# Hourglass attention and a gated MLP: the last value chunk of batch 0 on another DMA queue, shorter filler matmuls, and the first weights in smaller transfers

## The chip, the core and the metric

The kernel runs on one core of a Trainium2 chip. The core has a matmul engine (TensorE, PE in the profile; its weight loads are PEld), three engines for elementwise work (VectorE or DVE, ScalarE or ACT, GpSimd or POOL), and SyncE (SP), which here only issues transfers. Each engine works through its own list of instructions in order. Sixteen DMA engines move data between HBM and SBUF, the memory on the chip; matmuls write PSUM, from which VectorE and ScalarE read. GpSimd's transfers can convert fp32 to bf16 on the way; SP's copy as they are.

The metric is the device time of one execution in microseconds. The kernel before has a median of 316.63 us in three runs (315.98 to 320.5).

## The reference

Eight batches of eight heads, 576 tokens, head size 64. Attention is the sum of two parts: one over the means of four neighbouring tokens, repeated fourfold, and one over tokens less than four apart. An MLP follows.

```python
def _attn_ref(q, k, v):
    q_d = q.reshape(B, H, Sd, factor, D).mean(axis=3)      # factor = 4; k_d, v_d alike
    out_d = sm_attn(q_d, k_d, v_d)
    out_up = np.repeat(out_d, factor, axis=2)
    mask = np.abs(pos[:, None] - pos[None, :]) < factor
    scores = np.where(mask, scale * np.matmul(q, k.transpose(0, 1, 3, 2)), -1000000000.0)
...
    return out_up + np.matmul(attn, v)

def _moe_ref(x, w_in, w_out):                              # x: 4608 x 512, d_ff = 2048
    h = x @ w_in
    g = h * (1.0 / (1.0 + np.exp(-1.702 * h)))
    return g @ w_out
```

## The kernel before

The 4608 tokens form nine groups of 512 for the MLP. For each group `mm1` (line 697) multiplies by w_in (line 682) and applies the gate with ScalarE, and `mm2` (line 714) multiplies by w_out (line 746) and stores the result. Attention of the next batch is cut into steps and put between the matmuls of the running group at written-out positions, so that from about 24 us on TensorE has a full list. Batch 0 has no such cover: its attention is written out ahead of the loop, lines 789 to 878, and the order of the lines is the order on every engine.

This opening is what the change touches. In its order:

- GpSimd issues the loads of q and k of batch 0 (`load_1`, two tiles each), then the values (`load_vb`, line 219: five chunks of 128 rows, each in two halves of 64 partitions, fp32 in HBM to bf16 in the tile `vb`), then w_in in four transfers of 512 columns (`load_w_in`), of which the first stands ahead of the rest of the opening and three behind `pool_qk`, then q and k of batch 1, the first half of w_out, and inside group 0 the values of batch 1 and the second half of w_out.
- TensorE first runs filler matmuls on zeros (`warm`, line 637: `n` matmuls of `cols` columns; with `z=wf` on an fp32 tile, where one matmul shows as two passes in the profile, otherwise bf16). Then come the local scores of head group 0 (`scores`, line 367), fillers, those of head group 1, the downsampled scores (line 379), fillers, `prep_vd_pe` (line 336: sums of four value rows by matmuls with the selection matrix `psel`; its first call needs chunks 0 to 3, its second chunks 3 and 4), and the products with the values: `av_local0` (line 511, all five chunks) and `av_down0` (lines 525, 534). The turn of the result into the layout of the MLP is `turned` (lines 576 and 587, with a copy by ScalarE), and then the first matmuls with w_in follow (line 682).
- VectorE turns q and k (`prep_1`, line 267), sums fours (line 286) and normalises (`normalise0`, lines 553 to 561).
- ScalarE builds `psel` (`end_psel`, lines 173 to 178), takes the exponentials (`exp_local`, line 417; `exp_down`, line 423), copies the sums of values (line 345) and the turned results (lines 599, 603).
- SP issues nothing until batch 2's values (`load_v`, line 203: fp32 into a tile `vf`, converted by an engine with `prep_v`, line 305). `load_v` takes a gate: a small copy into the tile that an engine makes first, so that the transfers, which write the same place, wait for it.

The tile `vb` of batch 0 also holds a column of ones, set by `fill`, so that the product gives the sums for the division.

Of the kernel before, what the change touches and what calls it, by code (L numbers as in the profile page):

```python
# [19 lines left out]
def kernel(  # L20
# [9 lines left out]
    nc = tc.nc  # L30
# [38 lines left out]
    PM = [psum.tile([128, 512], FP32, name=f"pm{i}") for i in range(2)]  # L69
# [8 lines left out]
    def pm_tile():  # L78
        turn["m"] += 1
        return PM[turn["m"] % 2]  # L80

    wz = consts.tile([128, 512], BF16, name="wz")
    wf = consts.tile([128, 512], FP32, name="wf")
    off = consts.tile([128, 60], BF16, name="off")
    psel = consts.tile([128, 7, 64], BF16, name="psel")
# [27 lines left out]
    def fill():  # L113
        nc.vector.memset(wz, 0.0)
        nc.vector.memset(wf, 0.0)
        for t in kdT:
            nc.vector.memset(t[:, SD:160, :], 0.0)
        for t in vbs:
            nc.vector.memset(t[:, :, :, 64:65], 1.0)
        for t in vds:  # L120
            nc.vector.memset(t[:, :, :, 64:65], 4.0)
        for t in es:
            nc.vector.memset(t[:, :, 300:304], 1.0)
        for t in eds:
            nc.vector.memset(t[:, :, 432:480], 1.0)


    def make_off():
        nc.vector.tensor_tensor(out=dm, in0=dm, in1=dm, op=ALU.mult)
        nc.vector.tensor_single_scalar(out=dm, in_=dm, scalar=9.5, op=ALU.is_lt)  # L130
        nc.vector.tensor_scalar(
            out=off, in0=dm, scalar1=-1.0, scalar2=1e6, op0=ALU.add, op1=ALU.mult
        )
# [13 lines left out]
    def make_bias():  # L147
        nc.vector.memset(bias[:, 3:4], -3.0)
        nc.vector.tensor_copy(out=bias[:, 0:2], in_=rv)
        nc.vector.tensor_scalar(  # L150
            out=bias[:, 0:2], in0=bias[:, 0:2], scalar1=-1.0, scalar2=400.0,
            op0=ALU.add, op1=ALU.mult,
        )
# [17 lines left out]
    def end_psel():  # L171
        for m in range(7):
            nc.scalar.activation(
                out=dp[:, m], in_=di[:, 0:64], func=AF.Abs, scale=8.0, bias=db[:, m : m + 1]
            )
        nc.scalar.activation(out=dp, in_=dp, func=AF.Relu, bias=bias[:, 3:4])
        for sl, c in ((slice(0, 1), 1), (slice(1, 7), 0)):
            nc.scalar.activation(
                out=psel[:, sl], in_=dp[:, sl],
                func=AF.Exp, scale=-400.0, bias=bias[:, c : c + 1],  # L180
            )
# [21 lines left out]
    def load_v(b, gate=None, chunks=range(5)):  # L203
        t = ldp.tile([128, 5, H, D], FP32, name="vf", tag="vf")
        vf[b] = t
        if gate is not None:
            gate(t[0:1, 0, 0, 0:1])
        for i in chunks:
            for par in range(2):
                nc.sync.dma_start(  # L210
                    out=t[64 * par : 64 * par + 64, i],
                    in_=bass.AP(
                        tensor=v.tensor,
                        offset=v[b, 0].offset + (114 * i + KSTART[par]) * D,
                        ap=[[D, 64], [S * D, H], [1, D]],
                    ),
                )

    def load_vb(b, i):
        for par in range(2):  # L220
            nc.gpsimd.dma_start(  # L221
                out=vbs[b % 2][64 * par : 64 * par + 64, i, :, 0:D],
                in_=bass.AP(
                    tensor=v.tensor,
                    offset=v[b, 0].offset + (114 * i + KSTART[par]) * D,
                    ap=[[D, 64], [S * D, H], [1, D]],
                ),
            )
# [13 lines left out]
    def load_w_in(c, n):  # L242
        nc.gpsimd.dma_start(
            out=w_in_bf[:, :, c : c + n],
            in_=bass.AP(
                tensor=moe_w_in.tensor, offset=moe_w_in.offset + c,
                ap=[[d_ff, 128], [128 * d_ff, n_dmc], [1, n]],
            ),
        )
# [13 lines left out]
    def prep_1(name, b, qd):  # L263
        store, dst = {"k": (kf, kT), "q": (qf, qT)}[name]
        tt = work.tile([128, S, 2], BF16, name=f"{name}T{qd}", tag=f"{name}T{qd}", bufs=1)
        t32 = tt.rearrange("p t a -> p (t a)").bitcast(FP32)
        nc.vector.transpose(  # L267
            out=t32.rearrange("p (i c) -> p c i", c=18),
            in_=store[b, qd].bitcast(FP32).rearrange("p (c d) -> p c d", c=18),
        )  # L270
        dst[b, qd] = tt
# [10 lines left out]
    def reduce_qk(b, qd, name):  # L282
        t = kdT[qd][:, 0:SD, :] if name == "k" else new_qdT(b, qd)
        src = (kT if name == "k" else qT)[b, qd]
        with nc.allow_low_precision("the sum is rounded once, as the pairwise one is"):
            nc.vector.tensor_reduce(
                out=t, in_=src.rearrange("p (j f) a -> p j a f", f=4),
                axis=mybir.AxisListType.X, op=ALU.add,
            )
# [15 lines left out]
    def prep_v(b, eng, i=slice(0, 5), h=slice(0, H)):  # L305
        cp = eng.copy if eng is nc.scalar else eng.tensor_copy
        cp(out=vbs[b % 2][:, i, h, 0:D], in_=vf[b][:, i, h])  # L307
# [17 lines left out]
    def prep_vd_pe(b, pv, kcs=range(3), between=None):  # L325
        hp0, n = 0, HP
        vb, vd = vbs[b % 2], vds[b % 2]
        for kc, iis in ((0, (0, 1)), (1, (1, 2, 3)), (2, (3, 4))):
            if kc not in kcs:
                continue  # L330
            c0 = 256 * (kc - kcs[0])
            if between and kc == 1:
                between()
            for i in iis:
                for j in range(2):
                    nc.tensor.matmul(
                        pv[64 * j : 64 * j + 64, c0 : c0 + D * n],
                        lhsT=psel[:, PSEL.index((i, kc)), :],
                        rhs=vb[:, i, :, :].rearrange(
                            "p (hp j) d -> p hp j d", j=2  # L340
                        )[:, hp0 : hp0 + n, j, 0:D],
                        start=(i == iis[0]), stop=(i == iis[-1]),
                        tile_position=(0, 64 * j),
                    )
        nc.scalar.copy(
            out=vd[:, kcs[0] : kcs[-1] + 1, :, 0:D],
            in_=pv[:, 0 : 256 * len(kcs)].rearrange(
                "p (k h d) -> p k h d", k=len(kcs), h=HP
            ),
        )  # L350
# [26 lines left out]
    def score_d(b, qd, sd, kc, a, r):  # L377
        rows, j = slice(32 * r, 32 * r + 32), r % 2
        nc.tensor.matmul(  # L379
            sd[64 * j : 64 * j + 64, r // 2, SD * kc : SD * kc + SD],  # L380
            lhsT=kdT[qd][rows, 48 * kc : 48 * kc + 64, a],
            rhs=qdT[b, qd][rows, :, a],
            start=(a == 0), stop=(a == 1),
            tile_position=(32 * r, 64 * j),
        )
# [10 lines left out]
    def scores_d(b, qd, sd):  # L396
        for kc in range(3):
            for a in range(2):
                for r in range(4):
                    score_d(b, qd, sd, kc, a, r)  # L400
        return sd
# [13 lines left out]
    def exp_local(qd, sp):  # L415
        for u in range(2):
            nc.scalar.activation(  # L417
                out=es[2 * qd + u][:, :, 0:300], in_=sp[u][:, :, 0:300],
                func=AF.Exp, scale=inv_sqrt_d,
            )  # L420

    def exp_down(qd, sd):
        nc.scalar.activation(
            out=eds[qd][:, :, 0:432], in_=sd[:, :, 0:432],
            func=AF.Exp, scale=inv_sqrt_d / 16.0,
        )
# [210 lines left out]
    def warm(n, cols=512, t=None, z=wz):  # L637
        t = pm_tile() if t is None else t
        for _ in range(n):
            nc.tensor.matmul(  # L640
                t[:, 0:cols], lhsT=z[:, 0:128], rhs=z[:, 0:cols], start=True, stop=True
            )
# [150 lines left out]
    load_1("q", q, qf, 0, 1)  # L793
    iota_psel()
    fill()
    for i in range(5):
        load_vb(0, i)
    load_w_in(0, 512)
    warm(3, z=wf)
    warm(2)  # L800
    make_off()
    make_ident(di)
    make_psel()
    make_bias()
    end_psel()
    prep_1("k", 0, 0)
    prep_1("q", 0, 0)
    sp = scores(0, 0, PA[0:2])
# [4 lines left out]
    reduce_qk(0, 0, "q")  # L813
    pool_qk(0, 1, "q")
    reduce_qk(0, 1, "k")
    for c in range(1, 4):
        load_w_in(512 * c, 512)
    for qd in range(NQ):
        load_qk(1, qd)
    load_w_out(0)  # L820
# [1 line left out]
    warm(2, z=wf)  # L822
    sp = scores(0, 1, PA[0:2])
    exp_local(1, sp)
    exp_down(0, scores_d(0, 0, PA[2]))
    for hp in range(4):
        o[hp] = PA[hp % 3]
        y[hp] = y_tiles0()
    warm(1, z=wf)
    prep_vd_pe(0, PM[0], range(0, 2), lambda: warm(2, t=PM[1]))  # L830
    for hp in range(2):
        av_local0(hp, o[hp], range(5))
        normalise0(o[hp], y[hp], hp % 2, "a")
# [26 lines left out]
        copy_x(0, hp, PM if n is None else PA[n][:, :, 0:288])  # L860

    av_whole0(2)
    warm(1, t=PM[0], z=wf)
    turned(0, None)
    av_whole0(3)
    turned(1, 1)
# [90 lines left out]
```

## Time and profile before

| | us |
|---|---|
| median of three runs | 316.63 |
| the profiled execution, whole time | 317.56 |
| its span, first to last instruction | 315.8 |
| TensorE busy | 307.7 (97%) |
| ScalarE busy | 190.2 (60%) |
| GpSimd busy | 138.8 (44%) |
| VectorE busy | 123.5 (39%) |

Times in the profile are counted from the start of the span. The views used below are the page (busy time per engine; the span in 40 equal slices, each digit a busy share in tenths), the chain of work that ended last (start, length, what; each piece is what released the next), the timeline (start, length, engine, line, operation, tiles, count, and in brackets the idle time before it and what ended it), and the DMA view (queues, and for each kind of transfer the issuing queue, count, KB and the time from issue to landing). "issue" in the chain is time in which an engine waited for nothing that the profile shows. In the DMA view q0 holds GpSimd's transfers, q1 SP's, and q8 instructions.

### The profile page before, as it was taken

Reading aid. Unit: us, or ns where it says so; the run is one execution under the profiler, and the core shown is the slowest. Engines: PE = TensorE matmul, PEld = TensorE weight load, DVE = VectorE, ACT = ScalarE, POOL = GpSimd, SP = SyncE. Lnnn points to the kernel's source line nnn. Section 1 sums busy time; section 2 is a strip of 40 time slices with the busy share of each in tenths; the row PEclk is TensorE's granted clock in tenths of the full one; section 3 lists DMA queues with packets and bytes.
Section 4 is the critical chain, followed back from the end, with each engine's and each line's share of the span. In section 5 each row is a group of like instructions: output and inputs, shape, how many; then the busy total and the mean of one; then the engine's idle time right before and its main releaser. Section 6 shows DMA issues by size and latency. Waiting matters only on the chain.

```text
span 315.8 us, 10270 instructions
## 1 busy us (share of the span) xinstructions
PE 307.7 (97%) x4543; PEld 154.3 (49%) x4543; DVE 123.5 (39%) x247; ACT 190.2 (60%) x348; POOL 138.8 (44%) x170
## 2 busy tenths in 40 slices
PE   7989999999999999999999999999999999999995
PEld 3455455445544455455544554455445544444444
DVE  6763824720673057604760377027801640000000
ACT  5445882767657685668566856584767576316611
POOL 8863782179339920794079505960393000000000
PEclk9999999999999999999999999999999999999999
DMA  7999999999959913995299519971920110020011
GB/s 119 122 187 210 187 86 205 190 196 261 181 162 224 202 47 98 188 204 113 87 203 206 112 56 206 208 136 39 173 46 11 58 71 2 15 85 33 2 66 66
DMA packets 64075, 39.97 MB, mean 127 GB/s; under 512 B 44064, under 2 KB 55456, under 8 KB 64032
## 3 DMA queue, kind: packets, MB, share of 16 engines
q1 hardware_dynamic: 44496, 24.32, 36.0%
q0 software_dynamic: 19392, 14.95, 33.5%
q8 instruction: 35, 0.57, 0.8%
q14 instruction: 8, 0.07, 0.1%
q10 hardware_dynamic: 144, 0.07, 0.1%
HBM read 44.83 MB, written 9.44 MB: 172 GB/s over the span
## 4 chain that ended last, share of the span: by engine, by line
PE 91%; DMA 4%; ACT 1%; POOL 1%; issue 1%; DVE 0%; POOLq 0%; DVEq 0%; ACTq 0%
PE pm L746 36%; PE pm L682 35%; PE pa L682 4%; PE pa L367 2%; PE pa L439 2%; DMA qb<-in_q_dram 2%; PE pa L490 2%; PE pa L379 2%; PE pa L746 2%; PE pa L448 2%; DMA vb<-in_v_dram 1%; PE pm L761 1%; ACT od L610 1%; PE pm L640 0%; POOL vb L221 0%
## 5 line engine op out<-in xcount | busy, mean ns | idle before, releaser
L746 PE MATMUL pm<-w_out_bf,gT 128*128 128x512 bf16 x528 | 120.3, 380 | 0.0
L682 PE MATMUL pm<-xT,w_in_bf 128*128 128x512 bf16 x512 | 119.2, 379 | 0.5 <-ACT xT L603 0.3
L693 ACT ACTIVATE gT<-pm 128x512 bf16<-128x512 f32 x128 | 76.3, 598 | 43.7 <-PE pm L682 43.7
L682 PEld LDWEIGHTS <-w_in_bf 128*128 128x128 bf16 x576 | 55.7, 98 | 66.9 <-issue 1.1
L746 PEld LDWEIGHTS <-gT 128*128 128x128 bf16 x560 | 52.3, 98 | 60.7 <-issue 0.5
L431 DVE TENSOR_TENSOR es<-es,mask 128x600 bf16<-128x600 bf16 x28 | 19.0, 694 | 97.0 <-ACT es L417 96.3
L297 POOL TENSOR_TENSOR pq<-kT 128x576 f32<-128x576 bf16 x13 | 15.1, 1165 | 60.8 <-DVE kT L267 60.8
L731 ACT ACTIVATE osb<-pm 128x512 f32<-128x512 f32 (+2 forms) x35 | 20.4, 587 | 25.8 <-PE pm L746 23.0
L476 DVE TENSOR_TENSOR y<-pa,rc 128x896 bf16<-128x896 f32 x28 | 30.6, 1092 | 1.0
L480 ACT COPY y<-y 64x64 bf16<-64x64 bf16 x28 | 6.7, 241 | 31.3 <-DVE y L476 31.3
L417 ACT ACTIVATE es<-pa 128x600 bf16<-128x600 f32 x32 | 19.7, 668 | 8.7 <-PE pa L367 8.6
L313 POOL TENSOR_TENSOR v<-v 112x512 f32<-112x512 f32 x18 | 23.0, 1279 | 0.0
L307 POOL CAST vb<-vf 128x2560 bf16<-128x2560 f32 x6 | 13.9, 2318 | 19.8 <-DMA out_dram<-osb 6.3
L267 DVE STREAM_TRANSPOSE kT<-kb 128x576 f32<-128x576 f32 x16 | 19.9, 1246 | 5.8 <-DMA kb<-in_k_dram 5.6
L733 DVE TENSOR_SCALAR osb<-pm 128x128 f32<-128x128 f32 x1 | 0.3, 292 | 55.2 <-ACT osb L731 55.2
L632 DVE TENSOR_TENSOR xT<-pa,od 128x456 bf16<-128x456 bf16 (+2 forms) x84 | 16.6, 255 | 12.3 <-ACT od L610 12.1
L267 DVE STREAM_TRANSPOSE qT<-qb 128x576 f32<-128x576 f32 x16 | 19.9, 1243 | 0.8 <-DMA qb<-in_q_dram 0.4
L682 PE MATMUL pa<-xT,w_in_bf 128*128 128x512 bf16 x64 | 20.0, 379 | 0.0
L610 ACT COPY od<-pa 128x256 bf16<-128x256 bf16 (+1 forms) x56 | 18.3, 410 | 1.1 <-PE pa L490 0.4
L367 PEld LDWEIGHTS <-kT 32*64 32x64 bf16 x1280 | 14.2, 104 | 6.9 <-issue 4.1
L221 POOL DMA_DIRECT2D vb<-in_v_dram x20 | 13.7, 703 | 8.6 <-DMA w_in_bf<-in_moe_w_in_dram 3.6
L367 PE MATMUL pa<-qT,kT 32*64 32x60 bf16 x1280 | 16.5, 198 | 0.5 <-DVE qT L267 0.5
(90 smaller groups left out, 275.9 us busy)
## 6 DMA issues: line engine op xcount, KB each, us to landing
out_dram<-osb SPq DMA_DIRECT2D x35, 256.0 KB, 2.4
vf<-in_v_dram SPq DMA_DIRECT2D x60, 128.0 KB, 6.8
v<-in_v_dram SPq DMA_DIRECT2D x36, 192.0 KB, 5.4
kb<-in_k_dram POOLq DMA_DIRECT2D x16, 288.0 KB, 7.7
qb<-in_q_dram POOLq DMA_DIRECT2D x16, 288.0 KB, 8.9
w_in_bf<-in_moe_w_in_dram POOLq DMA_DIRECT2D x4, 512.0 KB, 9.2
w_out_bf<-in_moe_w_out_dram POOLq DMA_DIRECT2D x4, 512.0 KB, 12.5
vb<-in_v_dram POOLq DMA_DIRECT2D x20, 64.0 KB, 5.9
```

The source lines that it names most:

```text
L267: nc.vector.transpose(out=t32.rearrange("p (i c) -> p c i", c=18), in_=store[b, qd].bitcast(FP32).rearrange("p (c d) -> p c d", c=18),)
L313: eng.tensor_tensor(out=t1[0:112], in0=x[:, :, 0:2, :], in1=x[:, :, 2:4, :], op=ALU.add)
L367: nc.tensor.matmul(sp[r // 2][64 * par : 64 * par + 64, r % 2, 60 * i : 60 * i + 60], lhsT=kT[b, qd][rows, k0 : k0 + 64, a], rhs=qT[b, qd] ...
L417: nc.scalar.activation(out=es[2 * qd + u][:, :, 0:300], in_=sp[u][:, :, 0:300], func=AF.Exp, scale=inv_sqrt_d,)
L431: nc.vector.tensor_tensor(out=ev, in0=ev, in1=mask, op=ALU.mult)
L476: nc.vector.tensor_tensor(out=y.rearrange("p (x c) d -> p x c d", x=2), in0=ov[:, :, :, 0:D], in1=rc.to_broadcast([128, 2, 7, D]), op=ALU. ...
L610: nc.scalar.copy(out=od[:, 4 * t0 : 4 * (t0 + n)].rearrange("p (t f) -> p t f", f=4), in_=x[:, xx, c0 : c0 + n, None].to_broadcast([128, n ...
L632: nc.vector.tensor_tensor(out=sub(xT[hp], t0 + at, *dims), in0=sub(x, col, *from_x), in1=sub(od, at, *dims), op=ALU.add,)
L682: nc.tensor.matmul(acc, lhsT=w_in_bf[:, dmc, ffc * 128 : (ffc + 1) * 128], rhs=xT[dmc][:, g * TG : g * TG + TG], start=(dmc == 0), stop=(d ...
L693: nc.scalar.activation(out=gT[:, ffc, :], in_=acc, func=AF.Silu, scale=GELU_SCALE)
L731: eng.activation(out=osb, in_=ap, func=AF.Copy, scale=1.0 / GELU_SCALE)
L746: nc.tensor.matmul(ops[t], lhsT=gT[:, ffc, t * 128 : (t + 1) * 128], rhs=w_out_bf[:, ffc, :], start=(ffc == 0), stop=(ffc == n_ffc - 1),)
```

## The change

Six places change. `load_v` puts its gate into the first chunk that it loads, not always into chunk 0. Batch 0's values come by GpSimd for chunks 0 to 3 only; chunk 4 is loaded by SP as fp32 into the tile `vf`, behind a gate that ScalarE copies from `psel`, and ScalarE converts it into `vb` between `exp_local(1)` and `exp_down(0)`. The first 1024 columns of w_in come in four transfers of 256 columns, two at the place of the old first one, two behind `pool_qk`. Four fillers change: two bf16 matmuls of 512 columns become two of 256 ahead of the first scores; one fp32 matmul becomes two bf16 ones of 128 columns ahead of `prep_vd_pe`; the two of 512 inside it become two of 256; one fp32 matmul ahead of the first `turned` becomes two bf16 ones of 512.

```diff
         if gate is not None:
-            gate(t[0:1, 0, 0, 0:1])
+            gate(t[0:1, chunks[0], 0, 0:1])
...
-    for i in range(5):
+    for i in range(4):
         load_vb(0, i)
-    load_w_in(0, 512)
+    for c in range(2):
+        load_w_in(256 * c, 256)
     warm(3, z=wf)
-    warm(2)
+    warm(2, 256)
...
     end_psel()
+    load_v(0, lambda t: nc.scalar.copy(out=t, in_=psel[0:1, 6, 0:1]), [4])
     prep_1("k", 0, 0)
...
-    for c in range(1, 4):
-        load_w_in(512 * c, 512)
+    for c, n in ((512, 256), (768, 256), (1024, 512), (1536, 512)):
+        load_w_in(c, n)
...
     exp_local(1, sp)
+    prep_v(0, nc.scalar, 4)
     exp_down(0, scores_d(0, 0, PA[2]))
...
-    warm(1, z=wf)
-    prep_vd_pe(0, PM[0], range(0, 2), lambda: warm(2, t=PM[1]))
+    warm(2, 128)
+    prep_vd_pe(0, PM[0], range(0, 2), lambda: warm(2, 256, t=PM[1]))
...
     av_whole0(2)
-    warm(1, t=PM[0], z=wf)
+    warm(2, t=PM[0])
     turned(0, None)
```

## The prediction

> **What bounds the kernel now.** I read the page first. TensorE is busy 97% of the span and every later slice is full, so only the first slices hold time that this change can reach.
>
> ```profile
> span 315.8 us, 10270 instructions
> PE 307.7 (97%) x4543; PEld 154.3 (49%) x4543; DVE 123.5 (39%) x247; ACT 190.2 (60%) x348; POOL 138.8 (44%) x170
> PE   7989999999999999999999999999999999999995
> ```
>
> Next the chain of work that ended last, in order of time (start, length, what), for the opening:
>
> ```profile
> 3.87 6.83 DMA qb<-in_q_dram
> 10.71 0.28 issue
> 10.99 1.33 POOL vb L221 x2
> 12.32 4.30 DMA vb<-in_v_dram
> 16.66 0.24 PE pa L511 x4
> ...
> 20.01 1.06 PE pm L640 x2
> 21.07 0.25 PE pm L576 x3
> 21.45 1.11 issue
> 22.56 0.33 PE pm L587 x5
> ```
>
> Two stalls stand in it. TensorE starts the matmuls on chunk 4 at 16.66, when the last vb transfer lands (12.32 + 4.30 = 16.62). And at 21.45 it stops for 1.11 us in the middle of the eight matmuls of line 587, with "issue" in place of a releaser. The timeline of TensorE before the first stall:
>
> ```profile
> 13.68 1.12 PE L640 MATMUL pm<-wf 128*128 128x512 f32 x2
> 14.74 0.42 PE L336 MATMUL pm<-vb,psel 128*64 128x256 bf16 x4
> 15.09 0.60 PE L640 MATMUL pm<-wz 128*128 128x512 bf16 x2
> 15.62 0.53 PE L336 MATMUL pm<-vb,psel 128*64 128x256 bf16 x6
> 16.09 0.34 PE L511 MATMUL pa<-vb,es 64*64 64x65 bf16 x17
> 16.66 0.41 PE L511 MATMUL pa<-vb,es 64*64 64x65 bf16 x23 [0.24 <-DMA vb<-in_v_dram]
> ```
>
> So chunk 4 itself holds TensorE for 0.24 us; the rest of the time before it is fillers (L640). For the second stall I asked the DMA view for a stretch at a time. The instruction queue moves nothing from 13.5 to 20.0, then one packet of 16 KB:
>
> ```profile
> q8 instruction: 1, 0.02, 5.6%
> w_in_bf<-in_moe_w_in_dram POOLq DMA_DIRECT2D x1, 512.0 KB, 7.7
> ```
>
> The first line is the stretch 20 to 21 (5.6% of 16 engines for 1 us is 0.9 us of one engine); the second is the transfer issued at 12.99, which lands at 20.7. The whole run has 35 such packets for 9,086 matmuls and weight loads, 260 each, so they can only be mostly TensorE's instructions. My reading: the packet is asked for at the start of the previous block, on the av matmuls at 16.1, finds its engine inside the 512 KB transfer, is served as that ends, and TensorE goes on 1.5 us after it is in. A later pair looks the same: a packet in 51.2 to 52.1, and 0.26 us of "issue" at 53.31. None of this is labelled in the profile.
>
> **The change, step by step.**
>
> *Chunk 4 off GpSimd.* GpSimd loses two issues of line 221 (0.70 each) and gains two of line 243 (about 0.78 each): the same count, so everything from the batch 1 loads on keeps its place. This matters, because a GpSimd transfer waits for the one eight issues earlier: the eighth vb issue starts at 10.99 behind the qb transfer landed at 10.7 (3.87 + 6.8), the first w_out at 20.95 behind the first w_in at 20.7. Chunk 3's second half keeps its slot and its issue at 10.99. pool_qk starts after two w_in issues, about 13.2, instead of 13.88; nobody waits for it.
>
> *The gate and SP's two transfers.* ScalarE's copy (0.24, by the 64x64 copy of L480) runs at 8.3, in ScalarE's idle 0.89 us before 9.19; behind it stands only exp_local(0). SP has nothing before 52.7, so its two issues (0.73 each) end near 10. Landing: 6.8 us is the median of such rows under load, 5.5 the issue at 60.83, 3.3 the fastest vb. So 12 to 16; I take 13.5, since at 10 two queues share what one had and 256 KB are little. Cost on TensorE: none.
>
> *The cast.* 128x512 fp32 to bf16: the mask cast (L136, 128x600) took 0.69, so 0.6. It stands between exp_local(1), ending 14.15, and exp_down(0). Queued behind it are exp_down(0) (0.90) and the vd cast, which waits for TensorE until 16.20 anyway: 1.26 us of idle time hide 0.6. Without that cover (landing after 15.4) every further us of lateness moves av_down0 by one.
>
> *When vb chunk 3 is whole.* Now it decides. Its last half lands at 15.7 before (10.99 + 4.7). Unknown: the two SP transfers run ahead of it on the same 16 engines. If they use slack, 15.7; if they only push it, by their share, the 0.9 us that the last two vb took (15.7 to 16.6), 16.6. I take 16.2, between the two, as neither row is nearer. From there: the last L336 pair, then 20 matmuls of L511, 0.75 us to the first reciprocal against 17.00 now: 16.95. The step gains 0.05 (0.55 to minus 0.35).
>
> *Fillers.* Before scores(0, 0), two of 512 become 256: scores wait for qT (6.80 + 1.26 = 8.06), so at most 0.2, and nothing behind it. At 13.68 and 15.09 (1.12 and 0.60 by the rows) nearly all goes; this lies beside the wait for chunk 3, and counts nothing by itself. At 19.94 two fp32 passes, 0.43 apart, become two bf16 ones, 0.22 apart: 0.43 on the path. TensorE would reach line 587's fourth matmul at 21.45 - 0.43 - 0.05 = 20.97.
>
> *w_in in four.* The packet now meets a transfer of 256 KB. The first w_in took from 16.6 to 20.7 where the packet sits, so a half takes 2.0: from 16.2, ends at 18.2 and 20.2. The request is 16.5 or so; it may be served at the first end (in at 19.0, usable 20.5, no stall) or just miss it (served 19.7, usable 22.1). TensorE resumes at 20.97 or 22.1, against 22.56: 1.6 or 0.45 gained. I take the first, as the request lies more than a us before 18.2. The smaller rows: 64 KB vb transfers land 0.55 apart, 128 KB vf 0.65, 512 KB w_in 2.55. Time follows bytes above 128 KB, so two of 256 KB cost 0 to 0.3 more than one of 512; for both, plus chunk 4's doubled bytes, the DMA stream is later by 0 to 0.8, and I take 0.2.
>
> *What is late next.* From 24 to 50 TensorE is full, and the gain travels along to the third w_out chunk:
>
> ```profile
> w_out_bf<-in_moe_w_out_dram POOLq DMA_DIRECT2D x1, 512.0 KB, 6.9
> 50.59 1.89 PE L746 MATMUL pm<-w_out_bf,gT 128*128 128x512 bf16 x8
> ```
>
> That transfer is issued at 42.95 and lands at 49.8; its first reader starts at 50.59. It hangs on GpSimd's queue (vb issues from 40.94, behind the second w_out landed at 40.7), not on TensorE. So of any gain only 50.59 - 49.82 = 0.77 passes, less the 0.2 of a later stream: 0.55. Other slacks are wider: second w_out 1.5 (42.15 against 40.66), batch 1's last vb 1.5 (47.2 against 45.7), last w_out 3.0. Behind it the 0.26 at 53.31 should go too, since its packet is asked for earlier and TensorE waits meanwhile: 0.15 as an estimate between 0 and 0.26.
>
> **Sum.** 0.05 + 0.43 + 1.11 = 1.6 at 24 us, cut to 0.55 at 50.6, plus 0.15: 0.7 us, all of it kept to the end, where TensorE is the bound. The profiled execution took 317.56 (span 315.8 and 1.76 around it) and would take 316.86. It lies 0.93 above the median of the runs shown; from 316.63 the forecast is **315.9 us**.
>
> **Rivals.**
>
> *Nothing is left of it (0.30).* Chunk 3 lands at 16.6, the packet misses its gap, and the DMA stream is 0.8 later, so w_out comes at 50.6. Then 0.77 - 0.8 is nothing, and the time is 316.3 to 316.9: say 316.6. For it: the DMA row of the page is 9 in the slices 2 to 10. Against it: from 13.5 to 16 the DMA view gives 88 GB/s, and the windows 68 from 40 to 45, where later slices give 200; part of that is room, part the small packets. The Trainium skill ("DMA: Bandwidth & Descriptors", Issuing engines are not separate DMA queues) says that transfers from any engine run on the same 16 DMA engines and interleave, and that a second issuing engine saves issue time only. By that rule chunk 4 on SP frees nothing, which is this rival.
>
> *All of it arrives (0.18).* The third w_out does not hold TensorE, because the stream keeps its pace or runs ahead. Then 1.6 to 1.85 us: 314.9.
>
> *Slower: TensorE's clock (0.12).* Shorter fillers leave it nearly idle from 14.4 to 16.2. At the start a pass of 512 fp32 columns takes 0.85 us (starts 3.60, 4.46, 5.31), from 9.06 on 0.43: half the clock until some 5.7 us of matmuls had run. Should the quiet spell drop it again, up to 5.7 us of later work runs at half speed and loses up to 2.9; with half of the forecast kept, 318.6. It decides if about 2 us without dense work are enough. Against it: no such row after 9 us, though TensorE sat idle 1.1 us at 21.45. The Trainium skill ("TensorE: Matmul & The Clock Gate", Why this matters for your kernels) puts the limit at idle gaps of more than about 3 us. By that rule the clock stays, and this trace, whose longest idle time before the last matmul is 1.7 us at the start, agrees as far as it goes.
>
> **How the numbers follow.** Forecast 0.40, rivals 0.30, 0.18, 0.12. The range takes in the first three and part of the fourth, with the spread of a median: 314.6 to 317.7. Two per cent, 6.3 us, is about what a measurement of this kernel can tell from no change (its runs lie from 315.98 to 320.5). No case above reaches it; for the unforeseen I leave 0.01 faster and 0.03 slower, 0.96 within.
>
> **What would show it.** Right: L511 for chunk 4 with no DMA wait and the reciprocal at 17; the instruction packet before 19; no "issue" stall in line 587; L682 starting near 22.5 instead of 24.0; a DMA wait of half a us at the third w_out. Wrong: that packet still near 20, or matmuls of L511 or L682 at twice their present spacing.

## The result

The changed kernel takes 320.46 us (median of 22 runs, 319.15 to 321.76), the kernel before in the same comparison 316.54 (22 runs): a ratio of 1.0109, 95% interval 1.0094 to 1.0125. It is slower by 3.9 us by the medians and by 3.5 us by that ratio. The forecast was 315.9 us, 0.7 us faster than before, and its range ended at 317.7.

The profiled execution took 319.44 us with a span of 317.7. From its page (busy time of TensorE; the span in 40 slices; the granted clock in tenths):

```profile
span 317.7 us, 10278 instructions
PE 307.2 (97%) x4543; PEld 154.9 (49%) x4543; DVE 123.9 (39%) x247; ACT 190.9 (60%) x350; POOL 138.8 (44%) x170
PE   6779999999999999999999999999999999999995
PEclk9978999999999999999999999999999999999999
```

The busy time is what it was; the row of the clock shows what is new: 7 and 8 in the third and fourth slice. On the page of the kernel before the same row is

```profile
PEclk9999999999999999999999999999999999999999
```

The chain of work that ended last, for the opening (start, length, what):

```profile
3.87 7.01 DMA qb<-in_q_dram
10.88 0.28 issue
11.16 6.92 DMA vb<-in_v_dram
18.08 0.04 issue
18.12 0.30 PE pm L336 x2
18.43 0.50 PE pa L511 x34
...
24.60 0.51 PE pm L587 x8
...
27.45 0.59 PE pm L682 x2
```

Where the chain of the kernel before went on to the last transfer of chunk 4, it now hangs on the one ahead of that: the second half of chunk 3, issued at 11.16 (before 10.99), lands at 18.08 (before 15.7). All eight matmuls of line 587 now run in one piece; the 1.11 us of "issue" in their midst are gone. TensorE's timeline shows the wait (start, length, what, idle time and what ended it):

```profile
14.75 0.31 PE L336 MATMUL pm<-vb,psel 128*64 128x256 bf16 x2
15.27 0.31 PE L336 MATMUL pm<-vb,psel 128*64 128x256 bf16 x2 [0.21 <-DMA vb<-in_v_dram]
18.12 0.30 PE L336 MATMUL pm<-vb,psel 128*64 128x256 bf16 x2 [2.55 <-DMA vb<-in_v_dram]
18.36 0.57 PE L511 MATMUL pa<-vb,es 64*64 64x65 bf16 x40
...
26.56 0.59 PE L682 MATMUL pm<-xT,w_in_bf 128*128 128x512 bf16 x2
```

TensorE idles 2.55 us for chunk 3. Behind that the first matmul with w_in (L682) starts at 26.56 instead of 24.00, though 1.5 us of stall and filler are gone. The windows view tells why (stretch, its length, busy time and count of PE, PEld, DVE, ACT and POOL, then the granted clock, the DMA share and GB/s):

```profile
12.30:15.71 3.41, 2.76 (x116) 1.63 (x115) 2.25 (x2) 1.23 (x2) 3.27 (x5) 1.00 1.99 136
15.71:19.12 3.41, 1.00 (x46) 0.71 (x46) 0.23 (x2) 1.50 (x3) 3.41 (x6) 1.00 1.52 192
19.12:22.53 3.41, 3.41 (x77) 2.14 (x75) 2.71 (x8) 2.83 (x4) 2.07 (x4) 0.50 1.35 200
22.53:25.95 3.42, 3.42 (x64) 2.18 (x53) 2.20 (x5) 0.70 (x2) 1.17 (x2) 0.50 1.25 212
...
26.00:30.00 4.00, 3.71 (x46) 2.42 (x43) 2.38 (x4) 1.59 (x3) 1.50 (x3) 1.00 1.11 209
```

From 19.12 to 25.95 TensorE had half its clock, right behind a stretch in which it was busy for 1.00 of 3.41 us. Two causes, then: chunk 3 late, and the clock. Half clock for one such stretch of 3.41 us lowers the mean clock of a run by 0.5 * 3.41 / 317 = 0.0054, so a run's mean clock gives an estimate of how many it had: 0.995 one, 0.989 two, 0.984 three. (The traces show two and three; half clock behind the last matmul takes up to 0.002 more.) All 22 runs of the changed kernel lie at 0.982 to 0.989. Of the 99 runs of the kernel before whose clock is on record, in the comparisons below, 9 lie below 0.996 (median 320.2 us) and 90 above (median 316.7). As the drop is an effect of the change itself, the mean clock is given with the runs below, and "at full clock" means 0.996 or more.

Last, the DMA view of the three transfers that matter, one at a time, the second line with both of SP's (queue, count, KB, median us from issue to landing):

```profile
vf<-in_v_dram SPq DMA_DIRECT2D x1, 128.0 KB, 7.3
...
vf<-in_v_dram SPq DMA_DIRECT2D x2, 128.0 KB, 7.7
...
vb<-in_v_dram POOLq DMA_DIRECT2D x1, 64.0 KB, 6.9
```

SP's two, issued at 8.54 and 9.33, land at 15.8 and 17.5; the last half of chunk 3 takes 6.9 us where it took 4.7. Between 12 and 13 us, at the same view:

```profile
q1 hardware_dynamic: 340, 0.09, 95.3%
q0 software_dynamic: 241, 0.03, 88.4%
```

and in the kernel before, in the same microsecond:

```profile
q0 software_dynamic: 737, 0.09, 258.1%
```

GpSimd's queue (q0) got 241 packets through where it had 737 before; in the next two it had 413 and 467 (before 648 and 643), and SP's (q1) 353 and 276.

The order of issue tells the same. Around that time the value transfers of the changed kernel land in the order in which they were issued, whichever the queue: issued at 8.37 (GpSimd), 8.54 (SP), 9.04 (GpSimd), 9.33 (SP) and 11.16 (GpSimd), they land at 15.2, 15.8, 16.6, 17.5 and 18.1. So SP's two were issued, and landed, ahead of chunk 3's last half.

### The profile page after: what moved, and what is told of

Its sections match the earlier page's. It is cut to its first block, busy times and chain, and to the rows that moved or that the text cites. A ratio compares the mean times of both kernels' runs of the same rounds, so it can differ in the third digit from the quotient of the medians.

```text
span 317.7 us, 10278 instructions
## 1 busy us (share of the span) xinstructions
PE 307.2 (97%) x4543; PEld 154.9 (49%) x4543; DVE 123.9 (39%) x247; ACT 190.9 (60%) x350; POOL 138.8 (44%) x170
## 4 chain that ended last, share of the span: by engine, by line
PE 92%; DMA 4%; ACT 1%; POOL 1%; issue 1%; DVE 0%; POOLq 0%; ACTq 0%
PE pm L746 36%; PE pm L682 35%; PE pa L682 4%; PE pa L367 3%; DMA qb<-in_q_dram 2%; PE pa L439 2%; PE pa L379 2%; DMA vb<-in_v_dram 2%; PE pa L490 2%; PE pa L746 2%; PE pa L448 1%; PE pm L761 1%; ACT od L610 1%; PE pm L640 0%; PE pa L525 0%
## 5 line engine op out<-in xcount | busy, mean ns | idle before, releaser
L682 PE MATMUL pm<-xT,w_in_bf 128*128 128x512 bf16 x512 | 119.2, 379 | 0.5 <-ACT xT L603 0.3
L682 PEld LDWEIGHTS <-w_in_bf 128*128 128x128 bf16 x576 | 55.6, 98 | 67.0 <-issue 1.1
L431 DVE TENSOR_TENSOR es<-es,mask 128x600 bf16<-128x600 bf16 x28 | 18.9, 686 | 101.0 <-ACT es L417 100.1
L417 ACT ACTIVATE es<-pa 128x600 bf16<-128x600 f32 x32 | 19.7, 668 | 9.1 <-PE pa L367 9.0
L632 DVE TENSOR_TENSOR xT<-pa,od 128x456 bf16<-128x456 bf16 (+2 forms) x84 | 16.6, 254 | 12.4 <-ACT od L610 12.2
L307 POOL CAST vb<-vf 128x2560 bf16<-128x2560 f32 x6 | 13.9, 2321 | 16.6 <-DMA vf<-in_v_dram 11.8
L682 PE MATMUL pa<-xT,w_in_bf 128*128 128x512 bf16 x64 | 20.0, 379 | 0.0
L610 ACT COPY od<-pa 128x256 bf16<-128x256 bf16 (+1 forms) x56 | 18.3, 409 | 1.1 <-PE pa L490 0.4
L367 PE MATMUL pa<-qT,kT 32*64 32x60 bf16 x1280 | 16.6, 198 | 1.8 <-DVE qT L267 1.8
L367 PEld LDWEIGHTS <-kT 32*64 32x64 bf16 x1280 | 14.3, 104 | 8.2 <-issue 5.2
L221 POOL DMA_DIRECT2D vb<-in_v_dram x18 | 12.4, 704 | 8.6 <-DMA w_in_bf<-in_moe_w_in_dram 3.7
## 6 DMA issues: line engine op xcount, KB each, us to landing
w_out_bf<-in_moe_w_out_dram POOLq DMA_DIRECT2D x4, 512.0 KB, 11.5
```

The source lines that it names most:

```text
L367: nc.tensor.matmul(sp[r // 2][64 * par : 64 * par + 64, r % 2, 60 * i : 60 * i + 60], lhsT=kT[b, qd][rows, k0 : k0 + 64, a], rhs=qT[b, qd] ...
L417: nc.scalar.activation(out=es[2 * qd + u][:, :, 0:300], in_=sp[u][:, :, 0:300], func=AF.Exp, scale=inv_sqrt_d,)
L431: nc.vector.tensor_tensor(out=ev, in0=ev, in1=mask, op=ALU.mult)
L610: nc.scalar.copy(out=od[:, 4 * t0 : 4 * (t0 + n)].rearrange("p (t f) -> p t f", f=4), in_=x[:, xx, c0 : c0 + n, None].to_broadcast([128, n ...
L632: nc.vector.tensor_tensor(out=sub(xT[hp], t0 + at, *dims), in0=sub(x, col, *from_x), in1=sub(od, at, *dims), op=ALU.add,)
L682: nc.tensor.matmul(acc, lhsT=w_in_bf[:, dmc, ffc * 128 : (ffc + 1) * 128], rhs=xT[dmc][:, g * TG : g * TG + TG], start=(dmc == 0), stop=(d ...
```

## The experiments

In the diffs, "-" and "+" stand against the kernel named.

### Which of the three parts costs the time

Each part alone, on the kernel before. Fillers (all four shorter, nothing else):

```diff
-    warm(2)
+    warm(2, 256)
...
-    warm(1, z=wf)
-    prep_vd_pe(0, PM[0], range(0, 2), lambda: warm(2, t=PM[1]))
+    warm(2, 128)
+    prep_vd_pe(0, PM[0], range(0, 2), lambda: warm(2, 256, t=PM[1]))
...
-    warm(1, t=PM[0], z=wf)
+    warm(2, t=PM[0])
```

> The kernel before with only the four shorter fillers. Queue theory (the two SP transfers make chunk 3 late, and that is the loss): chunk 3 whole near 15.7 as before, granted clock 0.998, time 316.0 to 316.6. Clock theory (the shorter fillers let TensorE's clock drop): granted clock 0.982 to 0.989, a stretch of some 7 to 10 us in which matmuls are twice as far apart, time 318 to 319.5.

Measured: 317.71 us, ratio 1.0027 (0.9997 to 1.0058). Six of ten runs at full clock, median 316.4; four at 0.989 to 0.993, median 318.2. Its timeline:

```profile
14.93 0.31 PE L336 MATMUL pm<-vb,psel 128*64 128x256 bf16 x2 [0.26 <-DMA vb<-in_v_dram]
15.76 0.31 PE L336 MATMUL pm<-vb,psel 128*64 128x256 bf16 x2 [0.53 <-DMA vb<-in_v_dram]
15.99 0.83 PE L511 MATMUL pa<-vb,es 64*64 64x65 bf16 x40
```

Chunk 3 is whole at 15.7 as before, and from 9 us on no idle time in this trace is longer than 0.53 us. It is a trace at full clock; in four runs of ten the clock falls, so the shorter fillers alone can take away enough work for that. How long TensorE idled in those four isn't recorded. In its chain the eight matmuls of line 587 run in one piece, with w_in still in transfers of 512 columns.

Chunk 4 on SP, with its gate and cast, nothing else:

```diff
+    load_v(0, lambda t: nc.scalar.copy(out=t, in_=psel[0:1, 6, 0:1]), [4])
...
+    prep_v(0, nc.scalar, 4)
     exp_down(0, scores_d(0, 0, PA[2]))
```

> The kernel before with only chunk 4 on SP's queue and its cast by ScalarE; fillers as before, w_in in four transfers of 512 columns. Queue theory: the last half of chunk 3 lands near 18 (15.7 before), the products with the values start near 18.4, time 317.3 to 318.5 at a clock of 0.998. Clock theory: the long fillers hold the clock at 0.998 and the time stays within 0.5 of 316.5; if the wait for chunk 3 alone is enough to drop it, the clock shows 0.99 or less here too.

Measured: 320.67 us, ratio 1.0094 (1.0054 to 1.0135). Three runs at full clock, median 318.0; seven at 0.989 or less, median 320.9. This part alone carries nearly the whole loss, and both halves of it:

```profile
16.11 0.42 PE L336 MATMUL pm<-vb,psel 128*64 128x256 bf16 x4
18.34 0.31 PE L336 MATMUL pm<-vb,psel 128*64 128x256 bf16 x2 [1.81 <-DMA vb<-in_v_dram]
18.57 0.57 PE L511 MATMUL pa<-vb,es 64*64 64x65 bf16 x40
```

Chunk 3 ends the wait at 18.3, with the long fillers and the undivided w_in. So neither of these two made it late.

w_in's first 1024 columns in four, nothing else:

```diff
-    load_w_in(0, 512)
+    for c in range(2):
+        load_w_in(256 * c, 256)
...
-    for c in range(1, 4):
-        load_w_in(512 * c, 512)
+    for c, n in ((512, 256), (768, 256), (1024, 512), (1536, 512)):
+        load_w_in(c, n)
```

> The kernel before with only the first 1024 columns of w_in in four transfers of 256. Both theories: no loss, clock 0.998. My reading of the second stall: the instruction packet comes before 19 in place of 20.1, the 1.1 us of issue in the matmuls of line 587 is gone, and up to 0.77 of it passes the third w_out transfer: 315.7 to 316.3. If that reading is wrong the stall stays, and the time is 316.3 to 317.

Measured: 318.12 us, ratio 1.0057 (1.0025 to 1.0089), slower than either reading had it; eight of ten runs at full clock, median 317.9. The stall in line 587 is gone from its profile, with the long fillers in place. The division by itself gains nothing and seems to cost about 1 us. In its profile chunk 4 lands at 17.4 instead of 16.6; the profile also has longer "issue" stalls later, of 1.2 and 0.5 us between 80 and 100 us. Which of these the typical run has isn't known.

### Two parts at a time

The changed kernel with the long fillers back:

```diff
-    warm(2, 128)
-    prep_vd_pe(0, PM[0], range(0, 2), lambda: warm(2, 256, t=PM[1]))
+    warm(1, z=wf)
+    prep_vd_pe(0, PM[0], range(0, 2), lambda: warm(2, t=PM[1]))
```

(and the other two likewise).

> The changed kernel with the four fillers of before. Queue theory: chunk 3 is still late by 2.4 us, so most of the loss stays: 319 to 320. Clock theory: the clock is back at 0.998 and most of the loss is gone: 316.5 to 317.5.

Measured: 319.83 us, ratio 1.0111 (1.0058 to 1.0164), four runs: two at full clock, 318.4 and 318.6, two below, 321.1 and 321.5. Chunk 3 is whole at 18.0. Long fillers kept the clock in two of four runs; the late chunk stays.

The changed kernel with chunk 4 back on GpSimd:

```diff
-    for i in range(4):
+    for i in range(5):
         load_vb(0, i)
...
-    load_v(0, lambda t: nc.scalar.copy(out=t, in_=psel[0:1, 6, 0:1]), [4])
...
-    prep_v(0, nc.scalar, 4)
```

> The changed kernel with chunk 4 back on GpSimd's queue as bf16 (so the short fillers and the split w_in stay). By the runs so far the price of the SP part at full clock is 1.2 to 2 us (chunk 3 whole at 18 in place of 15.7), and the clock drop costs about 3 more where it happens. If both hold: chunk 3 whole near 16, some runs at a clock of 1.0 near 316 to 317 and some at 0.989 near 319, as with the shorter fillers alone. If the SP part were harmless, every run would show 0.98 to 0.99 and 319 to 321 as the changed kernel does.

Measured: 317.63 us, ratio 1.0027 (0.9991 to 1.0062); six runs at full clock, median 317.3, four below, median 318.9. Chunk 3 is whole at 15.5 and chunk 4 at 16.4. Taking this one part back removes most of the loss.

The changed kernel with w_in in four transfers of 512 again:

```diff
-    for c in range(2):
-        load_w_in(256 * c, 256)
+    load_w_in(0, 512)
...
-    for c, n in ((512, 256), (768, 256), (1024, 512), (1536, 512)):
-        load_w_in(c, n)
+    for c in range(1, 4):
+        load_w_in(512 * c, 512)
```

> The changed kernel with w_in in four transfers of 512 columns. If the split is worth something beside the other parts: slower than the changed kernel (320.5) by up to 1. If it costs, as the split alone did (317.9 at full clock against 316.6): 319.3 to 320.2. Clock 0.982 to 0.989 by either theory, as the quiet spell stays.

Measured: 321.1 us, ratio 1.0121 (1.0086 to 1.0156); all nine runs below full clock. Taking the division back removes none of the loss. Whether it costs something beside the other two parts, as it did alone, the intervals can't tell.

### Is it the clock

The changed kernel with 14 bf16 fillers of 512 columns in the wait for chunk 3, in place of the two of 256. Chunk 3 stays late; only TensorE is kept at work.

```diff
-    prep_vd_pe(0, PM[0], range(0, 2), lambda: warm(2, 256, t=PM[1]))
+    prep_vd_pe(0, PM[0], range(0, 2), lambda: warm(14, t=PM[1]))
```

> The changed kernel with fourteen bf16 fillers of 512 columns in place of two of 256 inside prep_vd_pe, so that TensorE works until about 17.5 while chunk 3 is on its way. Clock theory: every run or nearly every run at a clock of 1.0, chunk 3 still at 18, time 317.5 to 318.5. If the drop has another cause than the quiet spell, the clock stays at 0.98 to 0.99 and the time at 319 to 321.

Measured: 318.51 us, ratio 1.0054 (1.0025 to 1.0083). Nine of ten runs are at full clock, median 318.4. Timeline of its opening:

```profile
14.47 2.97 PE L640 MATMUL pm<-wz 128*128 128x512 bf16 x13 [0.16 <-issue]
17.37 0.42 PE L336 MATMUL pm<-vb,psel 128*64 128x256 bf16 x4
18.02 0.30 PE L336 MATMUL pm<-vb,psel 128*64 128x256 bf16 x2 [0.24 <-DMA vb<-in_v_dram]
18.26 0.57 PE L511 MATMUL pa<-vb,es 64*64 64x65 bf16 x40
...
23.95 0.38 PE L682 MATMUL pm<-xT,w_in_bf 128*128 128x512 bf16 x1
```

and its windows view, for the stretch in which the changed kernel has 0.50:

```profile
19.20:25.90 6.70, 5.84 (x143) 4.12 (x146) 5.88 (x15) 3.93 (x7) 3.07 (x5) 1.00 1.29 207
```

L511 starts where it did (18.26 against 18.36), but L682 starts at 23.95 instead of 26.56. Useless work put into a wait makes the kernel 2 us faster, 318.4 against 320.46; that is the clock's share. What stays, 318.4 against the 316.7 of the kernel before at full clock, is the late chunk's, net of what the other parts do.

The same with the cast of chunk 4 behind `exp_down(0)` instead of ahead of it:

```diff
-    prep_v(0, nc.scalar, 4)
     exp_down(0, scores_d(0, 0, PA[2]))
+    prep_v(0, nc.scalar, 4)
```

> The changed kernel with the wait filled (as in the run before, 318.5) and ScalarE's cast of chunk 4 moved behind exp_down(0). Chunk 4 lands at 17.5, so the cast held exp_down(0) from 14.2 to 18.1. If that is on the path beside chunk 3: av_down0 starts near 19.2 in place of 19.75 and the time falls by about 0.5 to 318.0. If chunk 3 alone sets the end: no difference, 318.3 to 318.7. Clock near 1.0 in most runs.

Measured: 318.18 us, ratio 1.004 (1.0019 to 1.006), all ten runs at full clock. In its profile L511 starts at 18.51 and L525 at 20.00 (18.26 and 19.75 with the cast ahead). No difference that can be measured: ScalarE is held up by the cast until 18.2, but chunk 3 holds TensorE as long anyway.

### What makes chunk 3 late: the bytes, the format or the place

Chunk 4 in fp32 with ScalarE's cast as in the change, but on GpSimd's queue behind chunk 3:

```diff
-    load_v(0, lambda t: nc.scalar.copy(out=t, in_=psel[0:1, 6, 0:1]), [4])
...
         load_vb(0, i)
+    load_v(0, None, [4], nc.gpsimd)
```

(`load_v` gets the issuing engine as an argument.)

> The changed kernel with chunk 4 still as fp32 and cast by ScalarE, but issued on GpSimd's queue behind chunk 3. If chunk 3 is late because the SP transfers run ahead of it on the same engines: chunk 3 whole at 15.7 to 16.3, chunk 4 at 17 to 17.8. If the fp32 form were slow in itself on any queue: chunk 4 about 2 us behind chunk 3; if only the mixing of two queues is: 1.3 us or less behind it. Time 318 to 320, since the cast then waits for chunk 4.

Measured: 319.82 us, ratio 1.0094 (1.0065 to 1.0124); all ten runs below full clock, so the time tells of the clock. The landings tell the rest: chunk 3 whole at 16.1, 2 us earlier than with the same bytes on SP. TensorE now waits for the cast:

```profile
16.13 0.31 PE L336 MATMUL pm<-vb,psel 128*64 128x256 bf16 x2 [0.70 <-DMA vb<-in_v_dram]
16.37 0.33 PE L511 MATMUL pa<-vb,es 64*64 64x65 bf16 x16
18.16 0.65 PE L511 MATMUL pa<-vb,es 64*64 64x65 bf16 x24 [1.46 <-ACT vb L307]
```

The longest idle time here is 1.46 us; the clock fell at 18.03 all the same. Here too the transfers land in the order of issue, chunk 4's halves at 16.6 and 17.4.

SP's two transfers, but issued behind chunk 3's second half, by a gate that GpSimd copies there:

```diff
-    load_v(0, lambda t: nc.scalar.copy(out=t, in_=psel[0:1, 6, 0:1]), [4])
...
         load_vb(0, i)
+    load_v(0, lambda t: nc.gpsimd.tensor_copy(out=t, in_=dr[0:1, 0:1]), [4])
```

> The changed kernel with the gate of SP's two transfers moved from ScalarE (8.3 us) to GpSimd, behind its issue of chunk 3's second half, so that they are issued at about 11.5 and 12.2 instead of 8.5 and 9.3. If chunk 3 was late because SP's packets stood ahead of it and took half of the engines' packets from 11.5 to 15, its last half lands at 15.7 to 16.4 instead of 18.1, and chunk 4 comes last, at 17 to 18.5; the quiet spell of TensorE is as long and its clock drops, so 319.5 to 321. If the price came from the extra bytes alone wherever they stand, chunk 3 stays at 17.5 or later.

Measured: 323.11 us, ratio 1.0197 (1.0154 to 1.024), all four runs at 0.983 to 0.984. The last half of chunk 3 in the DMA view, and the timeline:

```profile
vb<-in_v_dram POOLq DMA_DIRECT2D x1, 64.0 KB, 4.8
```

```profile
15.68 0.30 PE L336 MATMUL pm<-vb,psel 128*64 128x256 bf16 x2 [0.30 <-DMA vb<-in_v_dram]
15.91 0.33 PE L511 MATMUL pa<-vb,es 64*64 64x65 bf16 x16
20.49 0.35 PE L511 MATMUL pa<-vb,es 64*64 64x65 bf16 x9 [4.25 <-ACT vb L307]
```

Chunk 3 takes 4.8 us and is whole at 15.6, as before the change: SP's transfers ahead of it are what made it late. Issued behind it, at 11.74 and 12.52, they land at 17.3 and 19.7. The time is above the 319.5 to 321 expected because chunk 4 was expected by 18.5. TensorE idles 4.25 us and the half clock lasts 10.24 us (18.67 to 28.91).

SP's two transfers issued first of all, ahead of the loads of q and k, without a gate:

```diff
+    load_v(0, None, [4])
     load_qk(0, 0)
...
-    load_v(0, lambda t: nc.scalar.copy(out=t, in_=psel[0:1, 6, 0:1]), [4])
```

> The changed kernel with the SP transfers of chunk 4 issued first of all, without the gate. If their price is bytes on the same engines wherever they stand: q and k of batch 0 land about 1.3 us later, chunk 3 whole still near 17.7 to 18.2, time 320 to 322. If the price comes from two queues of small packets running against each other between 10 and 17: chunk 3 whole at 16.5 to 17.2, q and k late by 1 to 1.3.

Measured: 317.14 us, ratio 1.0003 (0.9971 to 1.0035); six runs at full clock, median 316.8, four at 0.994 to 0.995. SP's two land at 3.7 and 9.1, and chunk 3 in 5.9 us, whole at 16.8:

```profile
vb<-in_v_dram POOLq DMA_DIRECT2D x1, 64.0 KB, 5.9
```

The same bytes on the same queue cost no time that can be measured when they go where only q and k move, though the first scores (L367) then start at 9.16 instead of 8.30. That place alone, with long fillers and undivided w_in (the kernel before, chunk 4 on SP first of all):

```diff
+    load_v(0, None, [4])
     load_qk(0, 0)
...
-    for i in range(5):
+    for i in range(4):
         load_vb(0, i)
...
+    prep_v(0, nc.scalar, 4)
     exp_down(0, scores_d(0, 0, PA[2]))
```

> The kernel before with chunk 4 alone moved to SP, issued first of all with no gate: long fillers and w_in in four of 512 as before. With all three parts and the same early place the time was 317.14 and chunk 3 whole at 16.8. If the long fillers keep the clock at 1.0, all or nearly all runs stand at 0.998 or more, and the time is 316.3 to 317.3: no difference from the kernel before, for chunk 3 ends the wait where chunk 4 did. If the early place saved something that the other two parts gave back, it is 315.0 to 315.8 and the kernel beats both.

Measured: 316.79 us, ratio 0.9983 (0.9959 to 1.0008), all twelve runs at full clock. In its trace TensorE waits for no value chunk any more, neither 3 nor 4. But the scores come later, as q and k do (the downsampled ones, L379, at 13.80 instead of 13.18), the long fillers follow them, and L511 starts at 16.72, where the kernel before does its last L511 matmuls on chunk 4 from 16.66: no gain that can be measured.

### Was there anything to gain

The kernel before, profiled again, and the kernel before with the last filler alone shortened:

> The kernel before, profiled once more: does every execution have the 1.1 us stall inside the matmuls of line 587? If the stall belongs to the kernel, the instruction packet is near 20 and the stall about 1 us again. If it belongs to that one execution (317.56, when most take 316.4), the packet is near 18, there is no stall, and the first matmul with w_in starts near 23 in place of 24.0.

Measured: 317.78 us, span 316.0. The stall in the midst of line 587 is there again, 0.5 us, with the instruction packet at 19.6 to 20.5 and L682 at 23.45.

```diff
-    warm(1, t=PM[0], z=wf)
+    warm(2, t=PM[0])
```

> The kernel before with only the last filler shortened (one fp32 matmul to two bf16 ones ahead of the first turned), a candidate for a faster version. Its quiet spell before chunk 3 is filled as before, so the clock should stay at 1.0 as often as before. If its 0.43 us lies on the path: 316.0 to 316.4 against 316.6 to 316.8. If the instruction packet ends later anyway: no difference.

Measured: 316.63 us, ratio 0.9995 (0.9965 to 1.0024), all twelve runs at full clock. In its profile the stall of line 587 is gone, the packet comes at 17.9 to 18.8, and L682 starts at 22.64, though chunk 4 came at 17.1. So the trace shows the gain that the forecast counted, and the median doesn't. Nor can the missing stall be the shorter filler's doing: the packet was in at 18.8, and that filler runs only from 20.39. Of all traces here the stall stands in the two of the kernel before alone, with the packet at 20.1 and 19.6; in the fourteen others it starts between 17.2 and 18.8. Two of these, chunk 4 on SP alone (18.1) and SP first of all alone (17.9), have the long fillers and w_in in transfers of 512 columns. The two profiled runs of the kernel before, 317.56 and 317.78, lie a microsecond above its median; it may be that most of its runs have no such stall. That stays open.

## Why the prediction was wrong, step by step

**When vb chunk 3 is whole** is the step that failed first. The forecast put it at 16.2, between 15.7 and 16.6, and took for the upper bound the 0.9 us that the two removed transfers had taken. It landed at 18.1. That bound is the price of another exchange: the removed transfers, issued at 11.66 and 12.32, stood behind chunk 3, while SP's two, issued at 8.54 and 9.33, stand ahead of its last half. They are 256 KB of packets under 512 B, and they took 340, 353 and 276 packets of the three microseconds from 12 to 15; the last halves of chunks 2 and 3, which land from 14.7 to 15.7 in the kernel before, were due just behind. With the same bytes issued behind it (late gate) it came at 15.6, on GpSimd's own queue behind it at 16.1, with SP's two landed long before (early place) at 16.8, and with them just ahead at 18.0 to 18.3 in each of six versions. The first reciprocal, at 17.00 before and forecast at 16.95, came at 18.86: this term of the sum is 1.86 us lost, where it was put at 0.05 gained.

**The gate and SP's two transfers**: the gate ran at 8.33 for 0.19 us and the issues at 8.54 and 9.33, as forecast. The landing was forecast at 13.5, within 12 to 16; it was 17.5. The sentence "at 10 two queues share what one had and 256 KB are little" is the error: sharing was seen, its length was not worked out. At 0.09 MB a microsecond (340 packets) 256 KB take 3 us on half of the packets, and the first went out only after 11.5 (49 packets from 11.5 to 12), 3 us after the issue.

The Trainium skill ("DMA: Bandwidth & Descriptors", Issuing engines are not separate DMA queues) says that transfers of all issuing engines interleave on the same 16 engines. The counts above agree. It was used for the rival in which nothing is gained. What the runs add is that the place in the order decides: the same bytes moved from behind chunk 3 to ahead of it, and this made it worse than nothing.

**The cast**: 0.62 us against 0.6. It ran at 17.62, so the condition "landing after 15.4" held, the cover was gone, and `exp_down(0)` moved from 14.04 to 18.14. That every further microsecond moves `av_down0` by one was not added to the price, since chunk 3 held TensorE as long: with the cast behind `exp_down(0)` the time stayed.

**Fillers**: the working that their loss before `prep_vd_pe` "lies beside the wait for chunk 3, and counts nothing by itself" was right for time on the path and wrong for the clock. This step and the rival **Slower: TensorE's clock** belong together. That rival was given 0.12, and its mechanism is what happened: half clock behind a quiet spell, up to 2.9 us lost. The runs give 2.1 (320.46 against 318.4 with the wait filled), 2.9 (chunk 4 on SP alone, 320.9 against 318.0) and 1.8 (fillers alone). It said that about 2 us without dense work would decide; the trace has 2.55 us of idle time. Its time of 318.6 was too low because it kept half of the gain and had chunk 3 in time.

The Trainium skill ("TensorE: Matmul & The Clock Gate", Why this matters for your kernels) puts the limit at gaps of more than about 3 us, and by that rule the clock should have stayed. Here the measurement decides against it: in three of the four traces with a drop the longest idle time is shorter, 2.55 us (the changed kernel, where the clock fell in all 22 runs), 2.69 us (undivided w_in, all nine) and only 1.46 us (fp32 on GpSimd, all ten); the late gate alone, with 4.25 us, is beyond 3. The Trainium skill ("TensorE: Matmul & The Clock Gate", What's actually happening) also describes a free-running window of 3413 ns whose activity sets the clock, and with that the traces agree, as shown below.

**w_in in four**: the stall in line 587 is gone and the packet came at 18.55 to 19.45, near the 18.2 to 19.0 of the forecast. That the smaller transfers did it isn't shown: in every trace but the two of the kernel before it was gone too, whether w_in was divided or not and the last filler long or short, and the division alone was slower. The reading that the packet is served as the first w_in transfer ends fits only some traces. With transfers of 512 columns the packet was in at 21.0, 18.8 and 19.2 where that transfer landed at 20.7, 19.0 and 18.9 (the kernel before, last filler, fillers), but at 19.1 where it landed at 20.1 (chunk 4 on SP alone), and at 19.7 where it landed at 18.1 (SP first of all alone). What sets the packet's time stays open.

With this the largest term of the sum, 1.11 us, is in doubt. It was read from one execution that lay 0.93 us above the median, and then taken off the median; in medians no run here shows it as a gain.

**What is late next**: no gain reached 50 us in the changed kernel, so the wait for the third w_out wasn't put to the test there. **Chunk 4 off GpSimd** kept the queue's places as worked out.

The sum, in the profiles, up to L682: 24.00 + 1.86 (chunk 3) - 1.11 (stall) - 0.43 (filler) + 2.61 (clock, 26.56 against 23.95 with the wait filled) = 26.9; measured 26.56, so a further gain of 0.4 us is not accounted for. From L682 to the end of the span the kernel before takes 291.8 us and the changed one 291.1: the opening decides. In medians at full clock, 316.7 became 318.4 by the late chunk, net of whatever the other parts gain, and 320.5 with the clock.

## What to carry to other kernels

Before a transfer is moved to another queue, list which transfers are in flight at that time and which of them the next wait hangs on: here the moved one cost that wait 2.4 us when it was issued just ahead of it, and nothing measurable when it had landed long before. Issued behind it, it was itself what the next step waited for. Filler work in a wait is not free to remove: count TensorE's busy share over any 3.4 us, as the shorter fillers and the longer wait add up. Look at the granted clock of every run ahead of any other view when a small change costs more than the waits in its trace explain.

## What the runs showed of the hardware

Within each trace, the changes of the granted clock lie on a grid of 3.41 us: the full clock of the first stretch lasted 13.65 or 10.24 us in the traces with a drop (four or three times 3.41), and the half clock 6.83 or 10.24. Where the grid stands differs from run to run: the first full clock begins anywhere from 4.97 to 7.83 us. On this grid the four profiles with a drop have, in the piece just ahead of it, a busy share of TensorE (by the windows view) of 0.29 (changed kernel), 0.33 (fp32 on GpSimd), 0.20 (late gate) and 0.49 (undivided w_in). In the twelve profiles without a drop no piece after 9 us has less than 0.59. One before that, from 5.66 to 9.07 in the trace with SP first of all, has 0.46 and was passed over. So the limit seems to lie near half, but four drops don't fix it, and the early piece shows that the share of one piece isn't the whole rule. It would explain why the same kernel keeps its clock in some runs and loses it in others: the quiet spell can fall into one piece or be cut in two by the grid. In the trace with chunk 4 on SP alone, the wait of 1.81 us is cut at 17.39, the two pieces have shares of 0.70 and 0.65, and the clock stays; seven other runs of that kernel lost it. The late gate's trace, on its grid:

```profile
15.26:18.67 3.41, 0.68 (x20) 0.34 (x19) 0.00 (x0) 0.00 (x0) 3.41 (x6) 1.00 1.38 205
18.67:22.08 3.41, 1.59 (x44) 1.14 (x47) 1.09 (x4) 2.22 (x4) 2.16 (x4) 0.50 1.38 197
22.08:25.50 3.42, 3.42 (x76) 1.98 (x66) 2.40 (x7) 2.21 (x3) 1.01 (x3) 0.50 1.24 206
25.50:28.91 3.41, 3.41 (x53) 2.25 (x49) 1.98 (x6) 0.70 (x2) 1.24 (x2) 0.50 1.13 213
28.91:32.30 3.39, 3.09 (x36) 1.93 (x35) 3.39 (x5) 1.25 (x3) 2.29 (x3) 1.00 1.13 207
```

A piece with 0.68 us of work is followed by half clock; the next has 1.59 and keeps it; after two full ones the clock is back. By their mean clock, 9 of 99 runs of the kernel before had such a drop too: some of what looks like spread of an unchanged kernel is this clock.
